# Two more PSUM buffers for a matmul's output, paid for by pairing the accumulators, and a weight preparation moved and done in bf16

## Chip, cores and metric

The kernel runs on one core of a Trainium2 chip. The metric is device microseconds of one execution, as the median of several runs. A profile shows the span of one execution, which is 1.7 to 1.8 us shorter than the time of the same run. PE is the engine that does matmuls, ACT the one that does activations, DVE the vector engine. POOL issues the loads of x and f_logit, SP those of the weights and the stores. PSUM is the memory that the matmuls write into; a bank is, here, the place of one PSUM buffer.

## The reference

A gated recurrence over time, then a layer of two products whose larger one is taken element by element.

```python
sig = 1.0 / (1.0 + np.exp(-f_logit))          # f_logit, x: 4 x 6144 x 256
f = lower_bound + (1.0 - lower_bound) * sig
for t in range(S):
    h = f[:, t] * h + (1.0 - f[:, t]) * x[:, t]
    y[:, t] = h
h1, h2 = y @ w1, y @ w2                       # w1, w2: 256 x 1024
out = np.maximum(h1, h2) @ w_out              # w_out: 1024 x 256
```

## The kernel before

It uses max(h1, h2) = h1 + relu(h2 - h1). So out = relu(y (w2 - w1)) w_out + y (w1 w_out), and w13b = w1 w_out is made once at the start. Time is cut into 48 blocks of 512 steps. In each, PE transposes x and f_logit (tile tT), ACT takes a sigmoid (u), DVE makes the recurrence (ff, v, a scan into y), PE makes eight tiles dT = (w2 - w1) y, ACT empties each with a relu into rt, and PE adds rt w_out and y w13b into four accumulators psO, which DVE copies out (osb). The recurrence of block j+1 stands ahead of the matmuls of block j.

```python
    ps_t = tile_pool(name="ps_t", bufs=2, PSUM)    # tT, 128 x 512 bf16
    ps_d = tile_pool(name="ps_d", bufs=2, PSUM)    # dT, 128 x 512 f32
    ps_o = tile_pool(name="ps_o", bufs=1, PSUM)    # psO0..psO3, 128 x 256 f32 each
    ...
    # at the start, ahead of the recurrence of block 0: w1n, w2n, won are loaded in f32
    # 16 transposes of w1n (f32) -> dT -> ACT copies -> w1T (f32)
    # 16 matmuls w1T, won (f32) -> dT -> ACT -> w13b
    ...
    def moe(j):
        for fc in range(FC):                        # 8
            dT = ps_d.tile([P, TB], FP32, name="dT")
            for kc in range(KC):                    # 2
                nc.tensor.matmul(dT[:, :], lhsT=w21[:, kc, fc * P : (fc + 1) * P],
                    rhs=yk[kc][:, :], start=(kc == 0), stop=(kc == KC - 1))
            rt = rpool.tile([P, TB], BF16, name="rt")
            nc.scalar.activation(out=rt[:], in_=dT[:], func=AF.Relu)
            rts.append(rt)
        psos = [ps_o.tile([P, D], FP32, name=f"psO{i}") for i in range(NSB)]   # 4
        for fc in range(FC):
            for i in range(NSB):
                nc.tensor.matmul(psos[i][:, :], lhsT=rts[fc][:, i * TSB : (i + 1) * TSB],
                    rhs=wob[:, fc, :], start=(fc == 0), stop=False)
        # then 8 matmuls of y and w13b into psO, four DVE copies, two stores
```

The order of each engine's instructions is not that of the program text: it is set when the kernel is built, by the builder, the program that lays out each engine's instructions.

## Time and profile before

| | before |
|---|---|
| time, median (range) | 500.95 us (500.33 to 501.85, 13 runs) |
| span of the profiled run | 498.6 us |
| PE busy | 91% |
| length of a block, transposes to transposes | 9.79 us |
| first dT matmul of block 0 | 25.02 us |
| PE waiting for ACT's relu (its own idle time) | 20.1 us |

The lines behind it are in the prediction. To read it: busy shares say which engine to suspect, but the length of a block, taken from the start times in the timeline, says what the time is made of. A matmul's "duration" contains a tail that overlaps the next matmul (a dT matmul reads 377 ns, and the next one starts 216 ns after it), so idle time read from durations is too small.

### The profile page before, as it was taken

Reading aid. Unit: us, or ns where it says so; the run is one execution under the profiler, and the core shown is the slowest. Engines: PE = TensorE matmul, PEld = TensorE weight load, DVE = VectorE, ACT = ScalarE, POOL = GpSimd, SP = SyncE. Lnnn points to the kernel's source line nnn. Section 1 sums busy time; section 2 is a strip of 40 time slices with the busy share of each in tenths; the row PEclk is TensorE's granted clock in tenths of the full one; section 3 lists DMA queues with packets and bytes.
Section 4 is the critical chain, followed back from the end, with each engine's and each line's share of the span. In section 5 each row is a group of like instructions: output and inputs, shape, how many; then the busy total and the mean of one; then the engine's idle time right before and its main releaser. Section 6 shows DMA issues by size and latency. Waiting matters only on the chain.

```text
span 498.6 us, 8949 instructions
## 1 busy us (share of the span) xinstructions
PE 453.5 (91%) x3504; PEld 314.1 (63%) x3504; DVE 295.3 (59%) x485; ACT 269.8 (54%) x500; POOL 72.5 (15%) x102
## 2 busy tenths in 40 slices
PE   2899999999999999999999999999999999999996
PEld 1755765676667656756765676667567656766663
DVE  2466467656755675666467556756664666567451
ACT  3266456645654665466456546654664566466543
POOL 4121112112111211121111112111211111120000
PEclk9999999999999999999999999999999999999999
DMA  9947446745664675467456745754674566464112
GB/s 245 176 89 122 88 93 129 117 85 112 122 108 85 128 118 94 85 132 120 88 108 103 130 85 128 116 96 85 134 120 86 109 119 112 86 126 87 44 43 84
DMA packets 78698, 54.06 MB, mean 108 GB/s; under 512 B 3392, under 2 KB 78144, under 8 KB 78656
## 3 DMA queue, kind: packets, MB, share of 16 engines
q0 software_dynamic: 50688, 25.17, 40.2%
q1 hardware_dynamic: 27968, 28.32, 17.7%
q8 instruction: 27, 0.44, 0.4%
q14 instruction: 15, 0.12, 0.1%
HBM read 53.48 MB, written 25.17 MB: 158 GB/s over the span
## 4 chain that ended last, share of the span: by engine, by line
PE 55%; ACT 26%; DVE 9%; issue 6%; DMA 2%; ACTq 0%; POOL 0%; DVEq 0%; POOLq 0%
PE psO L222 29%; PE dT L209 22%; ACT rt L217 17%; DVE osb L241 9%; ACT u L170 9%; DMA fn<-in_f_logit_dram 2%; PE psO L231 2%; PE dT L106 1%; PE dT L91 0%; ACTq L217 0%; PE tT L164 0%; POOL xn L136 0%; PE tT L158 0%; ACTq L170 0%; DVEq L279 0%
## 5 line engine op out<-in xcount | busy, mean ns | idle before, releaser
L209 PE MATMUL dT<-y,w 128*128 128x512 bf16 x768 | 212.6, 377 | 29.2 <-ACT rt L217 20.1
L217 ACT ACTIVATE rt<-dT 128x512 bf16<-128x512 f32 x384 | 216.5, 600 | 35.8 <-PE dT L209 34.8
L222 PE MATMUL psO<-wob,rt 128*128 128x256 bf16 x1536 | 214.4, 272 | 0.0
L222 PEld LDWEIGHTS <-rt 128*128 128x128 bf16 x1536 | 149.6, 97 | 53.7
L241 DVE COPY osb<-psO 128x256 f32<-128x256 f32 x192 | 68.1, 418 | 164.2 <-PE psO L231 164.2
L170 ACT ACTIVATE u<-tT 128x512 bf16<-128x512 bf16 x96 | 52.4, 595 | 172.7 <-DVE osb L241 164.7
L209 PEld LDWEIGHTS <-w 128*128 128x128 bf16 x768 | 72.2, 97 | 107.5 <-issue 59.8
L191 DVE TENSOR_TENSOR_SCAN y<-ff,y,v 128x512 bf16<-128x512 bf16 x88 | 112.5, 1278 | 1.5
L136 POOL DMA_DIRECT2D xn<-in_x_dram x48 | 35.8, 746 | 373.7 <-PE tT L164 364.1
L181 DVE SCALAR_TENSOR_TENSOR v<-u,om,tT 128x512 bf16<-128x512 bf16 x96 | 69.4, 723 | 0.0
L172 DVE TENSOR_SCALAR ff<-u,lbm 128x512 bf16<-128x512 bf16 x96 | 46.5, 485 | 20.2 <-ACT u L170 20.2
L231 PE MATMUL psO<-w13b,y 128*128 128x256 bf16 x384 | 49.8, 273 | 0.0
L231 PEld LDWEIGHTS <-y 128*128 128x128 bf16 x384 | 37.6, 98 | 4.3
L158 PE MATMUL tT<-ident_b,xn 128*128 128x128 bf16 x384 | 37.6, 221 | 2.7 <-DMA xn<-in_x_dram 2.7
L164 PE MATMUL tT<-ident_b,fn 128*128 128x128 bf16 x384 | 37.8, 221 | 2.3 <-DMA fn<-in_f_logit_dram 2.3
L140 POOL DMA_DIRECT2D fn<-in_f_logit_dram x48 | 36.5, 760 | 1.8 <-PE dT L209 1.3
L158 PEld LDWEIGHTS <-xn 128*128 128x128 bf16 x384 | 27.7, 99 | 4.3 <-DMA xn<-in_x_dram 3.1
L164 PEld LDWEIGHTS <-fn 128*128 128x128 bf16 x384 | 25.8, 99 | 2.7 <-DMA fn<-in_f_logit_dram 2.6
L91 PE MATMUL dT<-ident,w1n 128*128 128x128 f32 x16 | 4.1, 423 | 6.6 <-DMA w1n<-in_moe_w_dram 6.6
L191 DVE TENSOR_TENSOR_SCAN y<-ff,v 128x512 bf16<-128x512 bf16 x8 | 9.7, 1217 | 0.2
L91 PEld LDWEIGHTS dT<-ident,w1n 128*128 128x128 f32 x16 | 3.1, 226 | 6.6 <-issue 6.6
L106 PE MATMUL dT<-won,w1T 128*128 128x256 f32 x32 | 7.1, 381 | 0.0
(16 smaller groups left out, 17.9 us busy)
## 6 DMA issues: line engine op xcount, KB each, us to landing
out_dram<-osb SPq DMA_DIRECT2D x96, 256.0 KB, 2.3
xn<-in_x_dram POOLq DMA_DIRECT2D x48, 256.0 KB, 4.9
fn<-in_f_logit_dram POOLq DMA_DIRECT2D x48, 256.0 KB, 5.6
w1n<-in_moe_w_dram SPq DMA_DIRECT2D x1, 1024.0 KB, 5.2
w2n<-in_moe_w_dram SPq DMA_DIRECT2D x1, 1024.0 KB, 8.6
won<-in_moe_w_out_dram SPq DMA_DIRECT2D x1, 1024.0 KB, 14.2
lbc<-in_lower_bound_dram SPq DMA_DIRECT2D x1, 1.0 KB, 2.1
```

Of the source, the lines that this page charges most:

```text
L140: nc.gpsimd.dma_start(out=fn[:], in_=f_logit[blk.b, blk.t0 : blk.t0 + TB, :].rearrange("(i p) d -> p i d", p=P),)
L158: nc.tensor.transpose(tT[:, i * TSB : (i + 1) * TSB], blk.xn[:, i, h * P : (h + 1) * P], ident_b[:],)
L164: nc.tensor.transpose(tT[:, TB + i * TSB : TB + (i + 1) * TSB], blk.fn[:, i, h * P : (h + 1) * P], ident_b[:],)
L170: nc.scalar.activation(out=u[:], in_=fT, func=AF.Sigmoid, scale=-1.0)
L172: nc.vector.tensor_scalar(out=ff[:], in0=u[:], scalar1=lbm1[:, h : h + 1], scalar2=1.0, op0=ALU.mult, op1=ALU.add,)
L181: nc.vector.scalar_tensor_tensor(out=v[:], in0=u[:], scalar=om[:, h : h + 1], in1=xT, op0=ALU.mult, op1=ALU.mult,)
L191: nc.vector.tensor_tensor_scan(out=y[:], data0=ff[:], data1=v[:], initial=init, op0=ALU.mult, op1=ALU.add,)
L209: nc.tensor.matmul(dT[:, :], lhsT=w21[:, kc, fc * P : (fc + 1) * P], rhs=yk[kc][:, :], start=(kc == 0), stop=(kc == KC - 1),)
L217: nc.scalar.activation(out=rt[:], in_=dT[:], func=AF.Relu)
L222: nc.tensor.matmul(psos[i][:, :], lhsT=rts[fc][:, i * TSB : (i + 1) * TSB], rhs=wob[:, fc, :], start=(fc == 0), stop=False,)
L231: nc.tensor.matmul(psos[i][:, :], lhsT=yk[kc][:, i * TSB : (i + 1) * TSB], rhs=w13b[:, kc, :], start=False, stop=(kc == KC - 1),)
L241: nc.vector.tensor_copy(out=osb[:, q, :], in_=psos[2 * g + q][:, :])
```

## The change

The four accumulators are put in pairs, two to a bank, so that psO takes two of the eight banks of the three pools instead of four (2 + 2 + 4 becomes 2 + 4 + 2); dT gets the other two, four buffers instead of two. That they had to be saved at psO is my understanding of it. In a pair only the first matmul carries the start flag. The preparation of w13b moves behind the recurrence of block 0 in the program and is done in bf16.

```diff
-    ps_d = ctx.enter_context(tc.tile_pool(name="ps_d", bufs=2, space=bass.MemoryType.PSUM))
+    ps_d = ctx.enter_context(tc.tile_pool(name="ps_d", bufs=4, space=bass.MemoryType.PSUM))
 ...
-    (w1n, w2n, w21, won, wob loaded and cast here; w1T and w13b made in f32)
+    def weight_prep():
+        (the same, and)
+        w1b = wpool.tile([P, KC, DFF], BF16)
+        nc.vector.tensor_copy(out=w1b[:], in_=w1n[:])
+        (transposes of w1b with ident_b, w1T in BF16, matmuls with rhs=wob)
+        return w21, wob, w13b
 ...
-        psos = [ps_o.tile([P, D], FP32, name=f"psO{i}") for i in range(NSB)]
+        pair = [ps_o.tile([P, 2, D], FP32, name=f"psO{g}") for g in range(NSB // 2)]
+        psos = [pair[i // 2][:, i % 2, :] for i in range(NSB)]
 ...
-                    start=(fc == 0),
+                    start=(fc == 0 and i % 2 == 0),
 ...
-                    stop=(kc == KC - 1),
+                    stop=(kc == KC - 1 and i % 2 == 1),
 ...
     recurrence(0)
+    w21, wob, w13b = weight_prep()
```

More of the change, by code (lines that the diff above doesn't have):

```diff
@@ L50 @@
     ps_t = ctx.enter_context(tc.tile_pool(name="ps_t", bufs=2, space=bass.MemoryType.PSUM))
-    ps_d = ctx.enter_context(tc.tile_pool(name="ps_d", bufs=2, space=bass.MemoryType.PSUM))
+    ps_d = ctx.enter_context(tc.tile_pool(name="ps_d", bufs=4, space=bass.MemoryType.PSUM))
     ps_o = ctx.enter_context(tc.tile_pool(name="ps_o", bufs=1, space=bass.MemoryType.PSUM))
-    ident = const.tile([P, P], FP32)
-    make_identity(nc, ident[:])
+    ident_f = const.tile([P, P], FP32)
+    make_identity(nc, ident_f[:])
     ident_b = const.tile([P, P], BF16)
-    nc.vector.tensor_copy(out=ident_b[:], in_=ident[:])
+    nc.vector.tensor_copy(out=ident_b[:], in_=ident_f[:])
     lbc = const.tile([P, KC], FP32)
@@ L71 @@
     )
-    w1n = wpool.tile([P, KC, DFF], FP32)
-    nc.sync.dma_start(out=w1n[:], in_=moe_w1.rearrange("(kc p) f -> p kc f", p=P))
-    w2n = wpool.tile([P, KC, DFF], FP32)
-    nc.sync.dma_start(out=w2n[:], in_=moe_w2.rearrange("(kc p) f -> p kc f", p=P))
-    w21 = wpool.tile([P, KC, DFF], BF16)
-    nc.vector.tensor_tensor(out=w21[:], in0=w2n[:], in1=w1n[:], op=ALU.subtract)
-    won = wpool.tile([P, FC, D], FP32)
-    nc.sync.dma_start(out=won[:], in_=moe_w_out.rearrange("(fc p) c -> p fc c", p=P))
@@ L82 @@
-    wob = wpool.tile([P, FC, D], BF16)
-    nc.vector.tensor_copy(out=wob[:], in_=won[:])
-    w1T = wpool.tile([P, FC, D], FP32)
-    for kc in range(KC):
-        for g in range(FC // 4):
-            pt = ps_d.tile([P, TB], FP32, name="dT")
-            for j in range(4):
-                fc = 4 * g + j
-                nc.tensor.transpose(
-                    pt[:, j * P : (j + 1) * P],
-                    w1n[:, kc, fc * P : (fc + 1) * P],
-                    ident[:],
-                )
-            for j in range(4):
-                fc = 4 * g + j
-                nc.scalar.copy(
-                    out=w1T[:, fc, kc * P : (kc + 1) * P], in_=pt[:, j * P : (j + 1) * P]
-                )
@@ L102 @@
-    w13b = wpool.tile([P, KC, D], BF16)
-    for kc in range(KC):
-        psw = ps_d.tile([P, TB], FP32, name="dT")
-        for fc in range(FC):
-            nc.tensor.matmul(
-                psw[:, 0:D],
-                lhsT=w1T[:, fc, kc * P : (kc + 1) * P],
-                rhs=won[:, fc, :],
-                start=(fc == 0),
-                stop=(fc == FC - 1),
-            )
-        nc.scalar.copy(out=w13b[:, kc, :], in_=psw[:, 0:D])
+    def weight_prep():
+        w1n = wpool.tile([P, KC, DFF], FP32)
+        nc.sync.dma_start(out=w1n[:], in_=moe_w1.rearrange("(kc p) f -> p kc f", p=P))
+        w2n = wpool.tile([P, KC, DFF], FP32)
+        nc.sync.dma_start(out=w2n[:], in_=moe_w2.rearrange("(kc p) f -> p kc f", p=P))
+        w21 = wpool.tile([P, KC, DFF], BF16)
+        nc.vector.tensor_tensor(out=w21[:], in0=w2n[:], in1=w1n[:], op=ALU.subtract)
+        w1b = wpool.tile([P, KC, DFF], BF16)
+        nc.vector.tensor_copy(out=w1b[:], in_=w1n[:])
+        won = wpool.tile([P, FC, D], FP32)
+        nc.sync.dma_start(
+            out=won[:], in_=moe_w_out.rearrange("(fc p) c -> p fc c", p=P)
+        )
+        wob = wpool.tile([P, FC, D], BF16)
+        nc.vector.tensor_copy(out=wob[:], in_=won[:])
+        w1T = wpool.tile([P, FC, D], BF16)
+        for kc in range(KC):
+            for g in range(FC // 4):
+                pt = ps_d.tile([P, TB], BF16, name="dT")
+                for j in range(4):
+                    fc = 4 * g + j
+                    nc.tensor.transpose(
+                        pt[:, j * P : (j + 1) * P],
+                        w1b[:, kc, fc * P : (fc + 1) * P],
+                        ident_b[:],
+                    )
+                for j in range(4):
+                    fc = 4 * g + j
+                    nc.scalar.copy(
+                        out=w1T[:, fc, kc * P : (kc + 1) * P],
+                        in_=pt[:, j * P : (j + 1) * P],
+                    )
+        w13b = wpool.tile([P, KC, D], BF16)
+        for kc in range(KC):
+            psw = ps_d.tile([P, TB], FP32, name="dT")
+            for fc in range(FC):
+                nc.tensor.matmul(
+                    psw[:, 0:D],
+                    lhsT=w1T[:, fc, kc * P : (kc + 1) * P],
+                    rhs=wob[:, fc, :],
+                    start=(fc == 0),
+                    stop=(fc == FC - 1),
+                )
+            nc.scalar.copy(out=w13b[:, kc, :], in_=psw[:, 0:D])
+        return w21, wob, w13b
@@ L200, in recurrence, with moe @@
         ys[j] = tuple(yh)
-    def moe(j):
+    def moe(j, w21, wob, w13b):
         blk = blocks[j]
@@ L222, in moe @@
                 nc.tensor.matmul(
-                    psos[i][:, :],
+                    psos[i],
                     lhsT=rts[fc][:, i * TSB : (i + 1) * TSB],
                     rhs=wob[:, fc, :],
-                    start=(fc == 0),
+                    start=(fc == 0 and i % 2 == 0),
                     stop=False,
@@ L231, in moe @@
                 nc.tensor.matmul(
-                    psos[i][:, :],
+                    psos[i],
                     lhsT=yk[kc][:, i * TSB : (i + 1) * TSB],
@@ L239, in moe @@
             osb = opool.tile([P, 2, D], FP32, name="osb")
-            for q in range(2):
-                nc.vector.tensor_copy(out=osb[:, q, :], in_=psos[2 * g + q][:, :])
+            for r in range(2):
+                nc.vector.tensor_copy(out=osb[:, r, :], in_=psos[2 * g + r])
             nc.sync.dma_start(out=out_rows(blk, 2 * g, 2), in_=osb[:])
@@ L252 @@
             recurrence(j + 1)
-        moe(j)
+        moe(j, w21, wob, w13b)
 _INS = ['x', 'f_logit', 'lower_bound', 'moe_w1', 'moe_w2', 'moe_w_out']
```

## The prediction

> **What bounds the kernel now.** I read the page's busy shares first, then the chain that ended last, then the groups, then the waits, and last the timeline of one block in the middle, which decided.
>
> ```profile
> span 498.6 us, 8949 instructions
> PE 453.5 (91%) x3504; PEld 314.1 (63%) x3504; DVE 295.3 (59%) x485; ACT 269.8 (54%) x500; POOL 72.5 (15%) x102
> PE 55%; ACT 26%; DVE 9%; issue 6%; DMA 2%; ACTq 0%; POOL 0%; DVEq 0%; POOLq 0%
> L209 PE MATMUL dT<-y,w 128*128 128x512 bf16 x768 | 212.6, 377 | 29.2 <-ACT rt L217 20.1
> L217 ACT ACTIVATE rt<-dT 128x512 bf16<-128x512 f32 x384 | 216.5, 600 | 35.8 <-PE dT L209 34.8
> ```
>
> PE is the busiest engine at 91%, yet ACT holds 26% of the chain. One line of PE idles: L209, which waits for L217, while L217 waits for L209. Two engines that wait for each other point to a short ring of buffers: dT has two PSUM buffers, PE fills one, ACT must empty it before PE may fill it again. The 29.2 us undercounts the loss, because a matmul's 377 ns includes a pipeline tail. So I count from starts, on PE in one block of the timeline (start, length to the end of the last, then what ended the idle time):
>
> ```profile
> 250.85 1.03 PE L209 MATMUL dT<-y,w 128*128 128x512 bf16 x4
> 252.28 0.59 PE L209 MATMUL dT<-y,w 128*128 128x512 bf16 x2 [0.40 <-ACT rt L217]
> 252.71 0.27 PE L222 MATMUL psO<-wob,rt 128*128 128x256 bf16 x1
> 252.81 0.59 PE L209 MATMUL dT<-y,w 128*128 128x512 bf16 x2
> 253.25 0.27 PE L222 MATMUL psO<-wob,rt 128*128 128x256 bf16 x1
> 253.61 0.59 PE L209 MATMUL dT<-y,w 128*128 128x512 bf16 x2
> 254.04 0.27 PE L222 MATMUL psO<-wob,rt 128*128 128x256 bf16 x1
> 254.15 0.59 PE L209 MATMUL dT<-y,w 128*128 128x512 bf16 x2
> 254.58 0.27 PE L222 MATMUL psO<-wob,rt 128*128 128x256 bf16 x1
> 254.95 0.59 PE L209 MATMUL dT<-y,w 128*128 128x512 bf16 x2
> 255.92 3.11 PE L222 MATMUL psO<-wob,rt 128*128 128x256 bf16 x27
> ```
>
> A dT matmul starts 0.216 us after the one before (four take 1.03: (1.03-0.377)/3); a psO matmul 0.109 (27 take 3.11: (3.11-0.272)/26). Four dT from 250.85 should end at 251.71; the next starts at 252.28: 0.57 lost. 253.25 plus 0.11 is 253.36, but the next dT starts at 253.61: 0.25 lost. 254.58 plus 0.11 is 254.69, the next is at 254.95: 0.26 lost. From 255.92 on there is no gap. So a block loses 1.08 us, all in its dT stretch. Its length, from the xn transposes at 249.95 to those at 259.74, is 9.79 us. The work alone is 16 x 0.216 + 40 x 0.109 + 16 x 0.055 (transposes: 0.22 us from group of four to group of four) = 3.46 + 4.36 + 0.88 = 8.70, and 8.70 + 1.08 = 9.78. It closes. The same count over the PE timeline of all 48 blocks gives 52 us of gaps ahead of dT matmuls, nearly the same 1.1 us in each.
>
> The waits hold one larger name, ACT's u for DVE's osb, 164.7 us. I do not believe it: u starts at 250.65, just after its transposes end (250.57), and in the next block the same idle time is put down to issue.
>
> [...] in the trace, two u in a row start 0.49 apart (251.14 less 250.65 in the chain). This decides whether ACT can keep up.[...]
>
> **The change, part by part.**
>
> (a) dT from two to four buffers. The two banks come from psO: four 1 KB accumulators, one bank each, become two pairs. Take t = 0 at a block's first transpose. Transposes to 0.88, then dT0..dT3 start at 0.88, 1.31, 1.74, 2.17, and PE wants dT4 at 2.61. ACT: u at 0.70 and 1.19 (250.65 less 249.95, then 0.49), relu0 at 1.67 (251.62), and each further relu 0.49 later while dT is ready. PE got the buffer of relu0 at 252.28, 0.66 after relu0's start. So buffers come free at 2.33, 2.82, 3.31, 3.80, and PE wants them at 2.61, 3.04, 3.47, 3.90: each is early, by 0.1 to 0.3 us, and earlier still for PE if psO matmuls lie between. No gap is left. Removed: 52 us; I leave 2 for odd blocks and a different order: -50.
>
> (b) The psO pairs: the same 40 matmuls and four copies a block. A copy may have to wait until both halves of its bank are done: two matmuls, 0.22 us later than now. The copies now end 0.97 us after t = 0; PE writes psO again at 2.3 or later. 0 on the path; perhaps +0.2 once, at the very end.
>
> (c) The preparation moves behind the first recurrence and goes to bf16. Now L106 takes 7.15 us for 32 matmuls of f32 (0.22 each), against 0.109 for the same shape in bf16 (L222): 3.5. The 16 transposes now take 1.94 for the first eight and 1.06 for each of two fours, 4.1 us; in bf16 16 x 0.055 plus a tail, 1.0. One more DVE cast (w1b) of 1.2 us, the duration of the wob cast of the same shape; one of two ACT table loads (1.3 us) goes. What of it is on the path? Now the first dT starts at 25.02, held by L106, 17.15 to 24.3. The data lands at 14.3 (fn) and 16.4 (won), which the change does not hasten: its loads stand on the same queues. After it, L106 could run from 17.7 (wob cast done) to 21.2, and the limit becomes y of block 0, now ready at 22.1 (scan at 20.90 for 1.22). First dT at about 22.1: -2.9. If DVE does the recurrence ahead of the casts, y comes at 20.1; if w21 (2.3 us) then follows it, dT waits until 22.4 and the rest of the preparation lies on PE's path in block 0, and the gain is 0. I take -2.5, give or take 2.5.
>
> Sum: 501.4 - 50 - 2.5 = 448.9; counted the other way, 47 x 8.70 + 7.8 (last block, no transposes) + 21.2 before the first block + 4.3 after PE's end (498.6 - 494.3) = 442.2 of span, plus 2.8 from span to the median time, 445.0, plus 2 for leftovers, 447.0. I say 448.
>
> **The rivals.** *ACT becomes the bound in the dT stretch.* It must pass two u and eight relu while PE does its dT. For it: it holds 26% of the chain, and one relu reads 600 ns. Were its cadence 0.60, u at 0.70 and 1.30, relu0 at 1.90, buffers free at 2.56, 3.16, 3.76, 4.36 against wishes of 2.61, 3.04, 3.47, 3.90: about 0.46 us of gap a block, 22 us in all, some 470. Against: two in a row start 0.49 apart, and psO matmuls can fill in. *Order.* The order of PE's instructions is set when the kernel is built; in the kernel before, psO matmuls already stand between dT ones. With four buffers the builder may put a psO matmul ahead of its rt, and PE waits in order: 0.1 to 0.25 us a block, 453 to 460. *A transfer or DVE becomes the bound.* A block needs 6.2 us of DVE (295.3/48) and 5.7 us of DMA (58% of 9.79), against 8.70 of PE; a load is issued about two blocks before use and lands in 5.6 us. I give this little: no change of the time until a block falls below 7 us. *The wait only moves,* to the psO matmuls, which need the last relu: PE would stand later for what it gains. Against: dT7 ends at about 4.3, relu7 ends by 5.8, and the 28 psO matmuls that come before the last four take 3 us, to 7.4.
>
> **Range and chances.** The floor is all gaps gone and the best start, 442 to 443. The middle rests on the gaps, which one block shows and all repeat. Upwards, a leftover of 0.2 us a block is 10 us: 458. The ACT rival, at one in ten, lies above that. Range 443 to 458. Faster than 491 (2%) needs only a fifth of the gaps: 0.96; within 2%: 0.035; slower: 0.005.
>
> **What would show it.** Right: a block of 8.7 to 8.8 us; "ACT rt" as a releaser of L209 falls from 20.1 to under 3; PE's busy sum falls by some 30 us, to 424 (6.7 of preparation and the 52 - 29 = 23 of pipeline tails that now stand in the gaps and are counted as busy), while its share rises to 95% or so; the first dT at about 22 us. Wrong: blocks at 9.2 with relu starts 0.6 apart (ACT rival), an idle time ahead of L222 (order, or the pairs' copies), fn or xn ahead of the transposes (transfers), or a first dT at 25 or later. A block that stays at 9.79 would say that the second dT buffer pair is not what PE waits for, and the whole would be wrong.

## The result

| | before | after |
|---|---|---|
| time, median (range) | 500.95 us | 445.59 us (445.24 to 446.74, 8 runs) |
| ratio, 95% interval | 1 | 0.8897 (0.8887 to 0.8907) |
| span | 498.6 us | 443.9 us |
| PE busy | 453.5 us, 91% | 425.2 us, 96% |
| length of a block | 9.79 us | 8.71 us |
| first dT matmul of block 0 | 25.02 us | 22.01 us |
| PE waiting for ACT's relu | 20.1 us | none listed |

A ratio is the mean time of one kernel's runs over that of the other's of the same rounds, so it is not quite the ratio of the two medians. Outputs were correct in all runs.

From the page of the changed kernel: the span, PE's busy time, the chain by engine, and the groups of relu and dT (busy us, mean ns of one, idle time before it and its releaser):

```profile
span 443.9 us, 8917 instructions
PE 425.2 (96%) x3488; PEld 310.7 (70%) x3488; DVE 296.0 (67%) x486; ACT 246.7 (56%) x500; POOL 72.1 (16%) x102
...
PE 95%; DMA 3%; ACT 1%; POOL 0%; issue 0%; DVE 0%; DVEq 0%; POOLq 0%
...
L221 ACT ACTIVATE rt<-dT 128x512 bf16<-128x512 f32 x384 | 193.6, 645 | 3.7 <-PE dT L213 3.7
...
L213 PE MATMUL dT<-y,w 128*128 128x512 bf16 x768 | 174.1, 379 | 0.0
```

The mutual wait of the prediction's first fence is gone on both sides: no idle time ahead of dT, and only one wait of relu, at the very start. The chain is now PE alone, 95%. The work of PE did not become faster (a dT matmul still shows 379 ns); the tails in the gaps are no longer counted as busy.

One block in the middle of the changed kernel, from the timeline (start, length, instruction):

```profile
230.49 1.42 DVE L246 COPY osb<-psO 128x256 f32<-128x256 f32 x4 [2.33 <-PE psO L236]
...
230.73 0.39 PE L162 MATMUL tT<-ident_b,xn 128*128 128x128 bf16 x4
...
231.43 1.08 ACT L174 ACTIVATE u<-tT 128x512 bf16<-128x512 bf16 x2 [3.71 <-issue]
...
231.62 3.62 PE L213 MATMUL dT<-y,w 128*128 128x512 bf16 x16
...
232.40 4.03 ACT L221 ACTIVATE rt<-dT 128x512 bf16<-128x512 f32 x8
...
235.08 3.66 PE L227 MATMUL psO<-wob,rt 128*128 128x256 bf16 x32
...
238.57 1.04 PE L236 MATMUL psO<-w13b,y 128*128 128x256 bf16 x8
...
239.44 0.39 PE L162 MATMUL tT<-ident_b,xn 128*128 128x128 bf16 x4
```

The 16 dT matmuls stand in one run, 0.216 us from start to start ((3.62 - 0.379)/15), then all 32 psO, then the eight with w13b, and the next block's transposes follow at once: 239.44 - 230.73 = 8.71. The psO matmuls that stood between the dT ones before have moved behind them, presumably because with four buffers free the builder had no dT to hold back. ACT's eight relu take 4.03 us, 0.48 from start to start ((4.03 - 0.645)/7, with the mean of the group), more than PE's 0.43 for one dT: within the stretch ACT falls behind PE, and four buffers are just enough to carry this. Experiments e4 and e7 test that.

### The profile page after: what moved, and what is told of

It is laid out like the page before. It is cut to its first block, busy times and chain, and to the rows that moved or that the text cites.

```text
span 443.9 us, 8917 instructions
## 1 busy us (share of the span) xinstructions
PE 425.2 (96%) x3488; PEld 310.7 (70%) x3488; DVE 296.0 (67%) x486; ACT 246.7 (56%) x500; POOL 72.1 (16%) x102
## 4 chain that ended last, share of the span: by engine, by line
PE 95%; DMA 3%; ACT 1%; POOL 0%; issue 0%; DVE 0%; DVEq 0%; POOLq 0%
PE psO L227 38%; PE dT L213 37%; PE psO L236 9%; PE tT L168 5%; PE tT L162 5%; DMA fn<-in_f_logit_dram 3%; PE dT L109 1%; ACT w1T L101 0%; ACT u L174 0%; POOL xn L140 0%; DVE osb L246 0%; DVEq L285 0%; POOL ident_f masks.py:199 0%; POOL ident_f masks.py:197 0%; POOLq masks.py:199 0%
## 5 line engine op out<-in xcount | busy, mean ns | idle before, releaser
L221 ACT ACTIVATE rt<-dT 128x512 bf16<-128x512 f32 x384 | 193.6, 645 | 3.7 <-PE dT L213 3.7
L227 PE MATMUL psO<-wob,rt 128*128 128x256 bf16 x1536 | 175.5, 273 | 0.0
L213 PE MATMUL dT<-y,w 128*128 128x512 bf16 x768 | 174.1, 379 | 0.0
L227 PEld LDWEIGHTS <-rt 128*128 128x128 bf16 x1536 | 150.3, 98 | 27.6
L213 PEld LDWEIGHTS <-w 128*128 128x128 bf16 x768 | 73.2, 98 | 79.5 <-issue 1.0
L236 PE MATMUL psO<-w13b,y 128*128 128x256 bf16 x384 | 49.8, 273 | 0.0
L162 PE MATMUL tT<-ident_b,xn 128*128 128x128 bf16 x384 | 38.0, 222 | 11.4 <-DMA xn<-in_x_dram 11.4
L236 PEld LDWEIGHTS <-y 128*128 128x128 bf16 x384 | 37.6, 98 | 4.3
L162 PEld LDWEIGHTS <-xn 128*128 128x128 bf16 x384 | 28.0, 99 | 12.8 <-DMA xn<-in_x_dram 11.4
L101 ACT COPY w1T<-dT 128x128 bf16<-128x128 bf16 x16 | 2.9, 364 | 10.9 <-PE dT L94 10.9
L109 PE MATMUL dT<-wob,w1T 128*128 128x256 bf16 x16 | 3.8, 415 | 1.9 <-ACT w1T L101 1.9
L109 PEld LDWEIGHTS <-w1T 128*128 128x128 bf16 x16 | 2.2, 142 | 3.0 <-ACT w1T L101 2.2
```

Source lines behind the costliest of these rows:

```text
L162: nc.tensor.transpose(tT[:, i * TSB : (i + 1) * TSB], blk.xn[:, i, h * P : (h + 1) * P], ident_b[:],)
L227: nc.tensor.matmul(psos[i], lhsT=rts[fc][:, i * TSB : (i + 1) * TSB], rhs=wob[:, fc, :], start=(fc == 0 and i % 2 == 0), stop=False,)
L236: nc.tensor.matmul(psos[i], lhsT=yk[kc][:, i * TSB : (i + 1) * TSB], rhs=w13b[:, kc, :], start=False, stop=(kc == KC - 1 and i % 2 == 1),)
```

## The experiments

Ten runs were made; e10 is the changed kernel again. They ran on three chips, each time beside the kernel before, which took 501.0, 501.3 and 500.7 us there. e1 to e3 take the change apart. With before and after they make a table:

| | f32 preparation, in front | bf16 preparation, behind |
|---|---|---|
| two dT buffers | 501.0 us (before) | 498.7 us (e2), with psO pairs 499.0 us (e3) |
| four dT buffers, psO pairs | 456.0 us (e1) | 445.6 us (after) |

### e1: the banks alone

```diff
 (the kernel before, with)
+ps_d bufs=4, and moe() of the changed kernel: pairs and start flags
```

> The PSUM part alone: four dT buffers and paired psO banks, the preparation left in f32 and ahead of the first recurrence as before. Theory (the gaps are waits for a dT buffer): blocks of 8.71 us as in the changed kernel, and about 52 of the 55 us of gain, so 448 to 449 us. Rival (a good share of the gain comes from the preparation, e.g. from a changed order of all that follows it): 455 or more.

Measured: 456.0 us (455.5 to 456.3), ratio 0.910 (0.9088 to 0.9113). By its number this is a miss, and it lies where the rival had put it (455 or more). The blocks answer: all regular blocks are 8.71 us long, as in the changed kernel, so the theory of the gaps holds. The loss is before them, and it is the rival's "changed order": the transposes that follow block 0's matmuls come at 40.95 us instead of 30.32. The timeline of PE shows why:

```profile
11.28 0.28 PE L158 MATMUL tT<-ident_b,xn 128*128 128x128 bf16 x2 [0.99 <-DMA xn<-in_x_dram]
16.65 9.43 PE L106 MATMUL dT<-won,w1T 128*128 128x256 f32 x32 [5.08 <-DMA won<-in_moe_w_out_dram]
25.91 0.28 PE L158 MATMUL tT<-ident_b,xn 128*128 128x128 bf16 x2
26.02 0.39 PE L164 MATMUL tT<-ident_b,fn 128*128 128x128 bf16 x4
...
30.89 1.28 PE L209 MATMUL dT<-y,w 128*128 128x512 bf16 x4 [0.70 <-DVE y L191]
```

After two transposes of block 0 stands the product w1T won. PE ran them in this order, so it stood still until won had landed (16.65), then did 9.43 us of f32 work, and only then the other transposes of block 0. In the kernel before, those run from 14.3 us on. The first dT comes at 30.89 us, 5.9 us later than in the kernel before. There, block 0's transposes stand between the parts of the preparation. That the builder put them there for want of a dT buffer, and with four had no need to, is my reading of it; that the order changed, and what it cost, the trace shows. So the two halves of the change don't add: the banks alone give 45.0 us, the preparation alone 2.3, both 55.4.

### e2 and e3: the preparation alone, and with pairs

```diff
 (e2: the changed kernel, with)
-ps_d bufs=4
+ps_d bufs=2, and moe() of the kernel before: four psO tiles
 (e3: the changed kernel, with)
-ps_d bufs=4
+ps_d bufs=2
```

> The preparation alone: bf16 and behind the first recurrence; two dT buffers and four psO banks as before. Theory: blocks stay at 9.79 us, the first steady block comes about 3 us earlier, so 497.5 to 498.5 us. Rival (preparation matters more): under 495. If its start hides behind the data that lands late: 501, no change.

> The changed kernel with the psO pairs but only two dT buffers (two PSUM banks lie idle). Theory: pairing by itself costs nothing on the path, since the copies only start some 0.2 us later and PE returns to psO over 1 us after they end: same time as the preparation alone (498), within 0.5 us. Rival (the pairs' copies hold PE, or the pairs themselves bring the gain): over 501, or under 490.

Measured: e2 498.74 us, ratio 0.9954 (0.9941 to 0.9966); e3 499.01 us, ratio 0.9962 (0.9950 to 0.9975). In both a block is 9.79 us again. e2 is just above the 497.5 to 498.5 expected; its second round of transposes starts 1.8 us earlier than before (32.01, from 33.80), not 3. The preparation saves 2.3 us where the order was good already, and pairing costs nothing that these runs can tell from zero. From e3 to the changed kernel the only edit is the number of dT buffers: 53.4 us. That is the gain of the buffers by themselves. From the first w13b matmul of the first block to that of the last, the traces have 460.35 and 408.89 us, so 51.5 of it lie there and 1.8 ahead of it, block 0's own gaps included (that first w13b matmul starts at 31.29 and 29.45).

### e4: three dT buffers

```diff
 (the changed kernel, with)
-ps_d bufs=4
+ps_d bufs=3
```

> The changed kernel with three dT buffers. The builder gives the same order of PE as with four (16 dT matmuls, then 40 psO). With relu starts 0.49 us apart and a buffer free 0.66 us after its relu's start, buffers come free at 2.33, 2.82, 3.31, 3.80, 4.29 us of the block, for dT3 to dT7, so dT7 starts at 4.29 instead of 3.90: 0.39 us a block, 8.71 + 0.39 = 9.10, in all 445.6 + 18.7 = 464 us. Rival (one spare buffer is enough, the loss with two came of the handover alone): within 3 us of the changed kernel. Rival (the ring hardly matters): near 498.

Measured: 463.24 us (462.96 to 463.59), ratio 0.9247 (0.9233 to 0.9261); blocks of 9.08 us, against 9.10 expected. One spare buffer is not enough. PE's busy share hides it well. From the page, the line of busy time, its group of dT, and, from the timeline, one block's dT stretch:

```profile
PE 442.5 (96%) x3488; PEld 309.4 (67%) x3488; DVE 296.3 (64%) x486; ACT 247.1 (54%) x500; POOL 72.0 (16%) x102
...
L213 PE MATMUL dT<-y,w 128*128 128x512 bf16 x768 | 191.2, 377 | 0.6 <-ACT rt L221 0.5
```

```profile
231.07 3.98 PE L213 MATMUL dT<-y,w 128*128 128x512 bf16 x16
```

PE reads 96% busy, the same share as in the changed kernel, and the dT group lists 0.6 us of idle time. But 16 dT take 3.98 us instead of 3.62: the 0.36 us are spread over five gaps, each shorter than the tail of the matmul before it (0.377 - 0.216 = 0.16 us), so they count as busy. What tells are the start times, the group's busy sum (191.2 instead of 174.1) and, in the first line, the share of PE's weight loads (PEld): 67%, where the changed kernel has 70% for the same weight loads.

### e5 and e6: which half of the preparation cures the start

```diff
 (e5: the changed kernel, preparation left in f32)
-w1b cast; transposes of w1b with ident_b; w1T BF16; rhs=wob
+transposes of w1n with ident_f; w1T FP32; rhs=won
 (e6: the changed kernel, preparation in front)
+    w21, wob, w13b = weight_prep()
     load_nat(blocks[0])
     ...
     recurrence(0)
-    w21, wob, w13b = weight_prep()
```

> The changed kernel with the preparation behind the first recurrence but still in f32: tells which half of the preparation saves the 10.5 us that the banks alone lost at the start. If the order does (PE stood ahead of the first transposes waiting for won): only the longer f32 matmuls remain on the path, L107 takes 7.15 instead of 1.75 to 3.5 us, first dT at about 25, so 448 to 449 us. If f32 does: 454 to 456.

> The changed kernel with the preparation in bf16 but written ahead of the first loads and recurrence, as in the kernel before. In its built order the transposes of blocks 0 and 0's second half stand ahead of the L109 matmuls (which wait for won), unlike in the banks-alone kernel. If the order of PE at the start is what counts: 446 to 448 us. If the place in the program counts whatever the built order: 454 to 456.

Measured: e5 449.39 us (448.62 to 449.50), ratio 0.8963; e6 447.04 us (446.36 to 447.13), ratio 0.8917. Blocks are 8.71 us in both. e6 lies in its range of 446 to 448, e5 a little above its 448 to 449, and far from the 454 to 456 of both rivals. Either half alone saves most of what e1 lost (6.6 and 9.0 of 10.4 us), which would be odd if f32 or the place in the program were the cause. The built order explains both: in e5 as in e6, block 0's transposes stand ahead of the product of w1T. From PE's timeline of e5, then of e6:

```profile
14.49 1.03 PE L166 MATMUL tT<-ident_b,fn 128*128 128x128 bf16 x8 [0.74 <-DMA fn<-in_f_logit_dram]
15.31 2.13 PE L92 MATMUL dT<-ident_f,w1n 128*128 128x128 f32 x9
17.23 8.31 PE L107 MATMUL dT<-won,w1T 128*128 128x256 f32 x32
```

```profile
14.36 0.61 PE L168 MATMUL tT<-ident_b,fn 128*128 128x128 bf16 x4 [2.44 <-DMA fn<-in_f_logit_dram]
...
17.87 3.57 PE L109 MATMUL dT<-wob,w1T 128*128 128x256 bf16 x16 [2.05 <-DVE wob L87]
```

In e5 the recurrence comes first in the program; in e6 presumably the longer way of the bf16 product (it needs wob, which DVE casts after won lands) put it back. What f32 costs once the order is good is e5 less after: 3 to 4 us.

### e7: how near ACT is to being the bound

```diff
 (the changed kernel, with)
-            nc.scalar.activation(out=rt[:], in_=dT[:], func=AF.Relu)
+            for hh in range(2):
+                cs = slice(hh * (TB // 2), (hh + 1) * (TB // 2))
+                nc.scalar.activation(out=rt[:, cs], in_=dT[:, cs], func=AF.Relu)
```

> The changed kernel with each relu as two instructions of 256 columns[...]. Tells how far ACT is from being the bound in the dT stretch (the rival of the prediction). Buffers free at 2.39, 2.95, 3.50, 4.06 against wishes of 2.61, 3.04, 3.47, 3.90: 0.13 to 0.16 us of gap a block, 446 + 7 = 453 us. If four buffers leave more slack than I think: 446. If ACT's rate were already the bound, the time would rise with ACT's whole added work, 8 x 0.065 x 48 = 25 us: 470.

Measured: 452.54 us (451.32 to 453.08), ratio 0.9026; blocks of 8.84 us. The expected 0.065 us more for a tile, on which its buffer times rest, was an estimate of mine that no run had shown. The timeline of the same kind of stretch (one of the 16 dT records, the first, is missing from the trace):

```profile
233.98 3.75 PE L213 MATMUL dT<-y,w 128*128 128x512 bf16 x15
...
234.75 4.54 ACT L223 ACTIVATE rt<-dT 128x256 bf16<-128x256 f32 x16
```

A tile now costs ACT 0.54 us, from (4.54 - 0.49)/15 = 0.27 us a half, 0.06 more than the 0.48 of one relu in the changed kernel. The eight tiles take it 4.54 us instead of 4.03, so ACT has 0.5 us more in a block, and the block grew by 0.13, as the ring's arithmetic had it (0.13 to 0.16). So ACT is not the bound (its whole added work would be 0.5 x 48, some 24 us), but it is close behind. The rival of the prediction was wrong about the rate, not about the mechanism.

### e8: two buffers, other work between

```diff
 (the changed kernel, with)
-ps_d bufs=4
+ps_d bufs=2
-rpool bufs=10
+rpool bufs=20
-        moe(j, w21, wob, w13b)
+        for fc in range(FC):
+            (dT and relu of block j, fc)
+            (the four psO matmuls of block j-1, fc)
+        (the w13b matmuls, copies and stores of block j-1)
```

> Only two dT buffers (with the pairs, so two PSUM banks idle), but PE's order changed: after each dT of block j come the four psO matmuls of one fc of block j-1, so PE has other work while ACT empties a buffer. If the gaps are the latency from a dT to its free buffer (0.43 + 0.25 + 0.66 = 1.34 us against 2 x 0.87 us of PE work per two buffers), they vanish without a third or fourth buffer: blocks of 8.71 us, 446 to 448 us (first block and last block lose a little overlap). If the ring of two is a limit by itself (each handover costs PE its 0.25 us): 9.7 a block, about 495.

Measured: 447.91 us (447.44 to 448.22), ratio 0.8936 (0.8921 to 0.8952); blocks of 8.71 us. PE, in a regular block:

```profile
230.85 0.59 PE L212 MATMUL dT<-y,w 128*128 128x512 bf16 x2
231.28 0.60 PE L225 MATMUL psO<-wob,rt 128*128 128x256 bf16 x4
231.72 0.59 PE L212 MATMUL dT<-y,w 128*128 128x512 bf16 x2
232.15 0.60 PE L225 MATMUL psO<-wob,rt 128*128 128x256 bf16 x4
```

With 0.87 us from dT to dT, two buffers are enough. So the loss was not that of a ring of two as such, but of a burst of dT work that PE does faster (0.43 us a tile) than ACT empties it (0.49). Two more buffers or an even mix cure it alike; the mix needs two dT buffers fewer and is some 2 us slower. The trace puts most of these 2 us ahead of the regular blocks: the first dT comes at 23.39 us (22.01 in the changed kernel), and block 0 has no psO matmuls of an earlier block to put between its dT.

### e9 and e10: a try at the start, and the changed kernel beside it

```diff
 (e9: the changed kernel, with load_nat(blocks[1]) behind weight_prep, and in load_nat)
+        if after is not None:                      # after = won, block 1 only
+            nc.gpsimd.tensor_copy(out=xn[:, 0, 0:1], in_=after[:, 0, 0:1])
+            nc.gpsimd.tensor_copy(out=fn[:, 0, 0:1], in_=after[:, 0, 0:1])
 (and in the last block two of the four osb copies on ACT)
```

> The changed kernel with a quicker start and end: the loads of block 1 wait until won has landed (a GpSimd copy of one column of won into their tiles ahead of the loads), so that block 0 and the weights share the DMA engines with 2 MB less; and in the last block ACT makes two of the four output copies. Theory (blocks are PE's floor of 8.71 us now, and only start and tail are left; the start waits for data at 11.4, 14.5 and 16.6 us): won lands at 11 to 13 us instead of 16.6, first dT at about 18, tail 0.4 shorter: 441 to 442 us. Rival (the start is bound by something else, or block 1 now comes too late): 445 or more.

> The changed kernel itself, as the neighbour of the quicker start on the same chip: 445 to 446.5 us.

Measured: e9 448.84 us (448.43 to 450.35), ratio 0.8966; e10 445.66 us (445.17 to 445.91), ratio 0.8894. The try made it 3 us worse. From the timeline of e9:

```profile
15.38 1.23 DVE L87 CAST wob<-won 128x2048 bf16<-128x2048 f32 x1 [2.67 <-DMA won<-in_moe_w_out_dram]
...
22.78 1.01 PE L165 MATMUL tT<-ident_b,xn 128*128 128x128 bf16 x8 [2.03 <-DMA xn<-in_x_dram]
```

won landed at 15.4 instead of 16.6, not at 11 to 13: holding back the loads of blocks 1 and 2 (POOL issues both only after won) hastened the rest by little over a microsecond. The first dT did come earlier, at 19.69. But block 1's x, issued only then, held PE until 22.78, where PE had the transposes of block 1 and, behind them in order, most of block 0's dT. The end gained nothing that shows. No kernel of this study beats the changed one, which took the same time again (e10).

## Why the prediction was right

The range of 443 to 458 holds 445.59; the point, 448, is 2.4 us high.

- **Gaps in the dT stretch, from a ring of two buffers that ACT empties.** Shown. The buffers alone, e3 to after, are worth 53.4 us; the count of gaps said 52, and the 50 booked left 2 for leftovers. There were none: the 8.70 us counted as PE's work is the block (8.71). This allowance is most of the 2.4 us. The second way of counting, 445.0 without it, was nearer, but in part by luck: its span, 442.2, was 1.7 short of the measured 443.9, and its step of 2.8 from span to time was 1.0 too much, for it set the span of a run of 500.33 us against the median of four runs (in one and the same run the two lie 1.7 to 1.8 apart).
- **The ring, step by step.** The same arithmetic (relu 0.49 apart, a buffer free 0.66 after its relu's start) gave 9.10 us a block for three buffers and, with the estimated 0.065 us more a tile, a gap of 0.13 to 0.16 (8.84 to 8.87 a block) for slower relus, both written down ahead of the runs; measured 9.08 and 8.84. Worked out afterwards for two, with the old order (one psO between, a relu 0.68 after its dT's start, 252.96 - 252.28): dT2 at 2.33 instead of 1.74, dT4 at 3.67 instead of 3.41, dT6 at 5.01 instead of 4.75, so 8.70 + 0.59 + 0.26 + 0.26 = 9.81; measured 9.79. This last case proves less than the other two: 0.66 and 0.68 were read from this very trace, 0.66 at the first of its gaps. That four leave no gap holds.
- **ACT as the bound.** Not so, but e7 shows it near. What decided this rival is that relus start 0.49 us apart (0.48 in the changed kernel) and not the 600 ns that the profile's page gives for one; the trace had it.
- **Order.** The worry was psO matmuls placed too early; the builder placed none between. The order mattered at another place, the start, which the prediction did not see.
- **The other rivals.** The wait did not move to the psO matmuls (no idle time is listed ahead of L227 or L236), and no transfer holds PE in the blocks: the transposes wait once for x and once for f_logit, at the start (11.4 and 0.8 us).
- **The pairs.** Predicted: copies 0.22 us later and nothing on the path. Before, they start 0.42 us after the first w13b matmul (249.50 and 249.08); after, 0.63 (230.49 and 229.86): 0.21 later. e3 shows no cost. Two groups in one bank with one start flag gave correct outputs in all nine kernels that use it (the changed one and all of e1 to e9 but e2); no run tries two flags in a bank.
- **The preparation, -2.5.** First dT predicted at about 22.1, measured 22.01; e2 is 2.3 us faster than before. That the sizes fit is in good part luck. Two steps were wrong and cancelled. L106's x32 are two records for each of 16 f32 matmuls (in bf16 the same line is x16), so the bf16 product should have been 16 x 0.109 = 1.7 us and not 3.5. And at the start a bf16 matmul of this shape does not take 0.109 but 0.21: 13 of them take 2.93 us (the fence below). The transposes in bf16 were to take 1.0 us and take 2.1 (L94), and no table load went: ACT still has both, at 0.74 and 13.21. The limit named, y of block 0 at 22.1, is not what held the first dT: that one needs only y's first half, scanned by 20.16, and it starts before the scan of the second half ends (22.06). PE was busy without a break from 17.99 until then, with L109 and the transposes of block 1, and the chain that ended last runs through these. With two buffers (e2) the first dT comes at 23.12. And as an independent term, 2.5 is wrong: beside four buffers, moving and casting is worth 10.4 us (e1 to after), because it also repairs the order that the buffers would spoil.
  From the changed kernel's timeline, the product of the preparation, the two scans of block 0 and the first dT, and the view by stretches of 17.9 to 20.7 us (length; busy time of PE, weight loads, DVE, ACT, POOL; granted clock; DMA share; GB/s):

```profile
17.99 2.93 PE L109 MATMUL dT<-wob,w1T 128*128 128x256 bf16 x13 [1.95 <-ACT w1T L101]
...
18.94 1.22 DVE L195 TENSOR_TENSOR_SCAN y<-ff,v 128x512 bf16<-128x512 bf16 x1
...
20.84 1.22 DVE L195 TENSOR_TENSOR_SCAN y<-ff,v 128x512 bf16<-128x512 bf16 x1
...
22.01 0.38 PE L213 MATMUL dT<-y,w 128*128 128x512 bf16 x1
```

```profile
17.90:20.70 2.80, 2.71 (x13) 1.90 (x14) 2.80 (x5) 1.22 (x6) 0.00 (x0) 1.00 1.45 196
```

  (2.93 - 0.415)/12 = 0.21, with 415 ns the mean of one L109; the same shape in the blocks has 273 ns and 0.109. The granted clock of that stretch reads 1.00, so it does not show this slow phase; the spacing does, and it is back at 55 ns for the transposes from 21.78 us on. No run here isolates the cause.
- **What would show it.** PE's busy time was to fall to 424: 425.2. "ACT rt" as releaser of dT under 3: none. The share of 95%: 96%.

## What to carry to other kernels

When two engines wait for each other over a small ring of buffers, count the gaps from start times on the bound engine: starts less the work's own spacing. Whether a ring is deep enough is then arithmetic with three numbers, the producer's spacing, the consumer's spacing and the delay from the consumer's start to the free buffer, and here it gave the block lengths for three and four buffers to 0.02 us ahead of the runs, and that for two afterwards, from the trace it was fitted on. Spreading the producer's burst made the blocks as short as deepening the ring did (e8). And a change of a buffer count can reorder code elsewhere that uses the same pool, as e1 shows (block 0's transposes of f_logit at 26.02 us there, from 14.29 in the kernel before): look at the start and the end as well as at the loop.
